# Regrouping the part-array matmuls of an attention round in a fused attention and expert kernel

## Chip, core and metric

The kernel runs on one core of a Trainium2 chip. The metric is the device time of one execution in microseconds (us); of several runs the median is given. The engines are TensorE (PE; its weight loads are listed as PEld), VectorE (DVE), ScalarE (ACT), GpSimd (POOL) and SyncE (SP, which only issues transfers).

## What is computed

Banded attention feeds a layer in which each token goes to one of eight experts. All data are float32.

```python
# q, k, v: (8 batches, 8 heads, 576 positions, 64); heads 0-3 plain window, heads 4-7 dilated
scores = q @ k.T / sqrt(64)
seen   = (0 <= i - j < 32)                                   # heads 0-3
seen   = (0 <= i - j < 128) and (i - j) % 4 == 0             # heads 4-7
x      = softmax(where(seen, scores, -1e9)) @ v              # -> (4608 tokens, 512)
logits = x @ w_gate                                          # (4608, 8)
e      = argmax(logits);  gate = softmax(logits)[e]
out    = gate * (relu(x @ w1[e]) @ w2[e])                    # w1[e]: 512x1024, w2[e]: 1024x512
```

## The kernel before

**Attention.** A unit is one pair of heads of one batch: 32 units, four to a batch, the first two of plain heads (`ty` 0), the last two of dilated ones (`ty` 1). A head's 576 queries are cut into nine blocks of 64, each with a band of 96 keys, so the matmuls are small and use only part of the 128x128 array of TensorE. A unit passes through these functions:

- `turn` (L293): transposes of q and of k into `turned`; a copy to qT on VectorE (L302), to kT on ScalarE (L304).[...]
- `front` (L340): 18 products of 64x64 weights with 96 columns (L360) into two banks `scores`. For the first four batches (`EARLY`), four matmuls put the mask into the banks ahead of them (L348), and VectorE takes the minimum from PSUM (L376); for later batches it adds the mask while it copies (L382, L389).
- `exponentials` (L393): nine or ten exponentials on ScalarE, with their sums.
- `norm` (L407): two small VectorE instructions, then a product on GpSimd (L412).
- `weights` (L416): nine transposes of the normed weights, three copies `eT` on VectorE (L424).[...]
- `summed` (L428), in two parts: 16 to 20 products with v, weights 96x64 (L437), into `xo`; ScalarE copies them to `xT` (L451, L458). An entry of the trace is half such a product[...], so a part shows 16 or 20 entries.
- `row_part` (L511): six transposes of `xT` into `xrow`[...], copied to `rows` by ScalarE and VectorE, then three products for the logits, weights 128x32 (L533).

`attention` (L463) is a software pipeline over rounds `i`. Round `i` holds, in this order: weights of unit i-2; norm of unit i-1; front of unit i; turns of unit i+1; rows and logits of unit i-3; exponentials of unit i; both parts of the sums of unit i-2. Matmuls of different kinds alternate through it. The next loads of q and k (`load_qk`) follow the turns and those of v (`load_v`) the sums, on SyncE's queue, which also issues the expert weights.

**Experts.** After the last unit of a batch, `route` (L541) finds each token's expert and writes its row to a bucket in memory; `tables` plans the slots of 128 rows that are then full. A slot (`moe`) is 32 products of 128x128 `ph` (L1183), each two entries in the trace, and eight of 128x512 `py` (L1215), likewise, with weights of 4 MB that SyncE fetches ahead. `xt` (L1108) is a turn of its rows.

**What sets the order.** `attention` and `moe` are generators. At each `yield cost, ended` of attention, the loop at the end hands out expert pieces by a clock of planned costs: `owed` grows with the cost times a rate, set from the slots that a routed batch makes ready, with due times from `ATT` = 32 and `BEHIND` = 12 (L1259). `ended` names a batch whose routing can begin. A round's costs sum to 6.6. Between two yields no expert piece is planned. A tile framework then orders the instructions of each engine by these priorities and by when it expects buffers and operands, so the built order departs here and there from the written one. All matmul results share seven PSUM banks.

## Time and profile before

| | |
|---|---|
| runs | 809.9, 810.85, 822.75 us; median 810.85 us |
| profiled execution | 815.9 us, its span 814.1 us |
| mean granted TensorE clock | 0.976 |
| PE, PEld busy | 766.0 us (94%), 559.6 us (69%) |
| DVE, ACT, POOL busy | 288.8 us (35%), 226.3 us (28%), 147.8 us (18%) |
| first, last sums (L437) | 31.1 us, 513.7 us |
| expert products ph, py busy | 274.3 us, 261.2 us |
| moved by transfers | 195.40 MB |

Busy is the time in which an engine executes. Matmuls overlap in the pipeline and their ends are modelled, so the time from the start of one group to the start of the next says more than a group's own duration. A timeline row gives start, duration, engine, line, tiles, weights and moving sizes, the count, and in brackets idle time ahead of it with what released it. The granted clock is the share of full speed that TensorE ran at.

### The profile page before, as it was taken

The page shows a single profiled execution, that of the slowest core. Times are in us where ns is not written, and L with a number is a line of the kernel's source. Part 1 is how long each engine was busy: PE and PEld are TensorE (multiplying, and loading weights), DVE is VectorE, ACT ScalarE, POOL GpSimd, SP SyncE. Part 2 cuts the span into 40 slices and gives each one's busy share as a digit, 9 for nine tenths or more (in the row PEclk, how much of TensorE's full clock was granted, in tenths as well). Part 3 has the DMA queues.
Part 4 walks back from the last instruction along what each step waited for, and adds up shares of the span by engine and source line. Part 5 has one row for each costly group of instructions (what it writes and reads, how often), then busy time and mean ns, then how long its engine had stood idle before and what let it go on. Part 6 is the DMA issues. An engine that isn't in the chain of part 4 may idle for free.

```text
span 814.1 us, 18002 instructions
## 1 busy us (share of the span) xinstructions
PE 766.0 (94%) x6838; PEld 559.6 (69%) x6838; DVE 288.8 (35%) x964; ACT 226.3 (28%) x853; POOL 147.8 (18%) x141
## 2 busy tenths in 40 slices
PE   4899978999999999999999999999999998999992
PEld 3777767777677777777777777776776472686770
DVE  2578857446333433336332452281010110111010
ACT  1687655343332333332322321100000000000100
POOL 0225423213111221113111130160000000000002
PEclk9699989999999999999999999999999999999997
DMA  9768799898998869968247477799980683883994
GB/s 209 168 139 214 182 304 305 189 305 278 307 268 316 292 217 308 297 205 269 71 147 248 143 210 263 253 362 350 323 283 27 217 273 130 311 279 135 316 330 159
DMA packets 165836, 195.40 MB, mean 240 GB/s; under 512 B 73520, under 2 KB 87600, under 8 KB 165746
## 3 DMA queue, kind: packets, MB, share of 16 engines
q1 hardware_dynamic: 153156, 169.00, 68.4%
q0 software_dynamic: 6992, 19.71, 6.7%
q10 hardware_dynamic: 5598, 5.48, 2.5%
q8 instruction: 57, 0.93, 0.5%
q14 instruction: 33, 0.27, 0.1%
HBM read 216.14 MB, written 22.59 MB: 293 GB/s over the span
## 4 chain that ended last, share of the span: by engine, by line
PE 44%; issue 36%; DMA 8%; DVE 5%; POOL 3%; ACT 3%; POOLq 0%; SPq 0%; ACTq 0%; DVEq 0%
PE ph L1183 13%; PE py L1215 12%; DMA x<-bucket 4%; PE xo L437 4%; PE weights L422 3%; PE scores L360 3%; POOL out_dram L1230 2%; ACT e L397 2%; PE xrow L523 2%; PE turned L319 2%; PE logits L533 1%; PE turned L311 1%; DMA k<-in_k_dram 1%; PE xt L1108 1%; DMA out_dram<-y,to 1%
## 5 line engine op out<-in xcount | busy, mean ns | idle before, releaser
L1183 PE MATMUL ph<-xt,w 128*128 128x128 f32 x2240 | 274.3, 277 | 0.0
L1183 PEld LDWEIGHTS ph<-xt,w 128*128 128x128 f32 x2240 | 261.6, 192 | 17.3 <-issue 14.4
L1215 PE MATMUL py<-w,h 128*128 128x512 f32 x560 | 261.2, 603 | 1.3 <-DVE h L1203 1.1
L1215 PEld LDWEIGHTS py<-w,h 128*128 128x128 f32 x560 | 99.3, 191 | 96.6 <-issue 89.4
L1230 POOL DMA_INDIRECT out_dram<-y,to x36 | 35.9, 998 | 376.7 <-ACT y L1226 356.1
L1226 ACT ACTIVATE y<-py,x 128x512 f32<-128x512 f32 x36 | 24.7, 685 | 228.4 <-PE py L1215 183.0
L412 POOL TENSOR_TENSOR e<-e,rec 128x864 f32<-128x864 f32 x32 | 52.2, 1631 | 170.0 <-DVE rec L411 103.7
L1110 DVE COPY xt<-xt 128x512 f32<-128x512 f32 x38 | 26.2, 690 | 151.1 <-PE xt L1108 151.0
L397 ACT ACTIVATE e<-e,lo 128x96 f32<-128x96 f32 x144 | 52.0, 363 | 73.9 <-DVE lo L389 73.6
L424 DVE COPY eT<-weights 96x384 f32<-96x384 f32 x96 | 48.7, 547 | 56.0 <-PE weights L422 55.2
L397 ACT ACTIVATE e<-scores,lo 128x96 f32<-128x96 f32 (+1 forms) x160 | 52.1, 344 | 28.1 <-DVE lo L376 21.2
L223 POOL DMA_INDIRECT bucket<-rows,idx x48 | 44.6, 930 | 54.5 <-DVE idx L622 32.6
L437 PEld LDWEIGHTS xo<-eT,v 96*64 96x64 f32 x1216 | 40.4, 140 | 18.9 <-issue 6.7
L437 PE MATMUL xo<-eT,v 96*64 96x64 f32 (+1 forms) x1216 | 46.8, 228 | 2.0 <-DVE qT L302 2.0
L1194 ACT ACTIVATE h<-ph 128x512 f32<-128x512 f32 x35 | 20.9, 597 | 89.5 <-PE ph L1183 83.3
L422 PE MATMUL weights<-ident,e 128*96 128x128 f32 x288 | 40.7, 291 | 3.4 <-POOL e L412 3.4
L422 PEld LDWEIGHTS weights<-ident,e 128*96 128x96 f32 x288 | 34.1, 135 | 9.3 <-issue 4.9
L1203 DVE TENSOR_SCALAR h<-ph 128x512 f32<-128x512 f32 x35 | 24.1, 690 | 40.9 <-PE ph L1183 40.8
L360 PEld LDWEIGHTS scores<-kT,qT 64*64 64x64 f32 x1152 | 33.8, 146 | 6.7 <-issue 3.8
L360 PE MATMUL scores<-kT,qT 64*64 64x96 f32 x1152 | 38.4, 265 | 0.0
L1227 DVE CAST to<-x 128x1 int32<-128x1 f32 x37 | 5.5, 149 | 92.7 <-DMA x<-bucket 78.0
L397 ACT ACTIVATION_READ_ACCUMULATOR e<-scores,lo 128x1 f32 (+1 forms) x160 | 33.3, 208 | 0.0
(210 smaller groups left out, 610.5 us busy)
## 6 DMA issues: line engine op xcount, KB each, us to landing
w<-in_moe_w_dram SPq DMA_DIRECT2D x164, 1024.0 KB
x<-bucket SPq DMA_DIRECT2D x26, 257.0 KB
v<-in_v_dram SPq DMA_DIRECT2D x32, 192.0 KB
q<-in_q_dram SPq DMA_DIRECT2D x32, 144.0 KB
q<-in_q_dram SPq DMA_DIRECT2D x8, 576.0 KB
v<-in_v_dram SPq DMA_DIRECT2D x48, 96.0 KB
k<-in_k_dram SPq DMA_DIRECT2D x28, 144.0 KB
k<-in_k_dram SPq DMA_DIRECT2D x7, 576.0 KB
```

Source lines behind the costliest of these rows:

```text
L223: nc.gpsimd.indirect_dma_start(out=bucket, out_offset=bass.IndirectOffsetOnAxis(ap=idx, axis=0), in_=rows, in_offset=None, bounds_check=NR ...
L360: nc.tensor.matmul(sc[r][64 * c : 64 * c + 64, 96 * (i % 5) : 96 * (i % 5) + 96], lhsT=qT[rows, 64 * j : 64 * j + 64], rhs=kT[rows, first_ ...
L397: nc.scalar.activation(out=e[p0:p1, i], in_=s[:, 96 * (i - i0) : 96 * (i - i0) + 96], func=AF.Exp, bias=lo[p0:p1, i : i + 1], scale=-1.0, ...
L412: nc.gpsimd.tensor_tensor(out=e, in0=e, in1=rec.unsqueeze(2).broadcast_to([128, 9, 96]), op=OP.mult)
L422: nc.tensor.transpose(tp[0:96, 128 * i : 128 * i + 128], e[:, a + i], ident)
L424: nc.vector.tensor_copy(eT, tp[0:96, 0:384])
L437: nc.tensor.matmul(xo[DH * h : DH * h + DH, at0 : at0 + nq], lhsT=vt[:, 2 * hl + r, j, :] if ty == 0 else vt[:, hl, j, DH * r : DH * r + D ...
L1110: nc.vector.tensor_copy(xt, ps)
L1183: nc.tensor.matmul(ph[:, fi], lhsT=w1[:, c, 128 * f : 128 * f + 128], rhs=xt[:, c], start=c == 0, stop=c == 3,)
L1215: nc.tensor.matmul(py, lhsT=h[:, f], rhs=w2[:, f], start=f == 0, stop=f == 7)
L1226: nc.scalar.activation(y, py, AF.Copy, scale=x[:, DM : DM + 1])
L1230: i = nc.gpsimd.indirect_dma_start(out=out, out_offset=bass.IndirectOffsetOnAxis(ap=to, axis=0), in_=y, in_offset=None, bounds_check=N - 1 ...
```

## The change

The order of a round in `attention` and the places of its yields. Now round `i` begins with norm of unit i-1, front of unit i, both parts of the sums of unit i-3 (a round later than before) and the logits of unit i-4, with no yield among them; then come weights of unit i-2, turns of unit i+1 and rows of unit i-3, and last the exponentials of unit i. `row_part` is split: its logits are a function of their own, `logit_part`, which runs a round after the rows. Routing of a batch begins behind its last logits. `load_v` goes with the sums. The planned costs become 3.0, 1.1, twice 0.5 and 0.65, together 5.75 a round; `ATT` and `BEHIND` stay. There are two rounds more, in which only the last units drain.

```diff
-        evs, dens, xT = {}, {}, None
-        for i in range(len(units) + LAG + 1):
-            if LAG <= i < len(units) + LAG:
-                eTs = weights(evs.pop(i - LAG))
-                yield 1.1, None
+        evs, dens, eTs, xTs = {}, {}, {}, {}
+        for i in range(len(units) + LAG + 3):
+            ended = None
             if 0 < i <= len(units):
                 norm(evs[i - 1], dens.pop(i - 1))
             if i < len(units):
                 evs[i], lo, places = front(qT["q"], qT["k"], units[i][1], units[i][0] < EARLY)
-            yield 1.1, None
+            u = i - LAG - 1
+            if 0 <= u < len(units):
+                b2, ty2, hl2 = units[u]
+                xTs[u] = pool.tile([128, S], F32, tag="xT", name="xT", bufs=3)
+                for part in range(2):
+                    summed(eTs[u], b2, xTs[u], ty2, hl2, part)
+                del eTs[u]
+                if hl2 == 1 and b2 + 1 < B:
+                    load_v(b2 + 1, ty2)
+            if 0 <= u - 1 < len(units):
+                b2, ty2, hl2 = units[u - 1]
+                logit_part(b2, 2 * ty2 + hl2, xTs.pop(u - 1))
+                ended = b2 if (ty2, hl2) == (1, 1) else None
+            yield 3.0, ended
+
+            if 0 <= i - LAG < len(units):
+                eTs[i - LAG] = weights(evs.pop(i - LAG))
+                yield 1.1, None
             if i + 1 < len(units):
...
                 for n in "qk":
                     qT[n] = turn(b2, ty2, hl2, n)
-                    yield 1.0, None
+                    yield 0.5, None
                 if hl2 == 1 and b2 + 1 < B:
                     load_qk(b2 + 1, ty2)
-            if i > LAG:
-                b2, ty2, hl2 = units[i - LAG - 1]
-                row_part(b2, 2 * ty2 + hl2, xT)
-                yield 0.9, b2 if (ty2, hl2) == (1, 1) else None
+            if 0 <= u < len(units):
+                b2, ty2, hl2 = units[u]
+                row_part(b2, 2 * ty2 + hl2, xTs[u])
+                yield 0.65, None
 
             if i < len(units):
                 dens[i] = exponentials(evs[i], lo, places)
-            if LAG <= i < len(units) + LAG:
-                b2, ty2, hl2 = units[i - LAG]
-                xT = pool.tile([128, S], F32, tag="xT", name="xT", bufs=3)
-                for part in range(2):
-                    summed(eTs, b2, xT, ty2, hl2, part)
-                    if part == 1 and hl2 == 1 and b2 + 1 < B:
-                        load_v(b2 + 1, ty2)
-                    yield 0.75, None
```

```diff
             )
+
+    def logit_part(b, c, xT):
         for j in range(3):
             nc.tensor.matmul(
                 logits[b][32 * j : 32 * j + 32],
```

## The prediction

> **What bounds the kernel now.** I read the page first, then the busy time by stretches, the waits, and the timeline of TensorE. On the page PE is busy 94% of the span, DVE 35%, ACT 28%, POOL 18%. The stretches say where that holds:

> ```profile
> 20.00:40.00 20.00, 16.60 (x190) 13.98 (x190) 10.95 (x30) 13.15 (x72) 4.90 (x3) 0.66 0.76 174
> 80.00:120.00 40.00, 34.22 (x530) 27.09 (x529) 30.07 (x101) 25.82 (x121) 14.63 (x13) 0.91 0.81 234
> 240.00:280.00 40.00, 40.00 (x352) 29.90 (x351) 13.57 (x41) 13.93 (x51) 5.23 (x4) 1.00 0.90 305
> 400.00:440.00 40.00, 40.00 (x365) 29.96 (x367) 13.49 (x30) 13.36 (x49) 5.25 (x4) 1.00 0.50 160
> ```

> The columns are the stretch, its length, busy us of PE, PEld, DVE, ACT and POOL, the granted clock, the DMA share and GB/s. Up to about 120 us attention runs alone, with DVE and ACT two thirds busy and PE with holes. From about 150 us on, expert slots stand between the attention pieces and PE never rests: what takes PE time off there shortens the span one for one, since ACT and DVE have two thirds of it free. Expert slots alone (from about 520 us) are full too.

> A busy PE is not PE at its best, so I take times from start to start. First the expert matmuls alone, then the same with attention among them:

> ```profile
> 561.84 3.74 PE L1183 MATMUL ph<-xt,w 128*128 128x128 f32 x32
> 565.42 7.03 PE L1215 MATMUL py<-w,h 128*128 128x512 f32 x16
> 572.29 2.95 PE L1183 MATMUL ph<-xt,w 128*128 128x128 f32 x25
> ```

> ```profile
> 299.83 0.80 PE L437 MATMUL xo<-eT,v 96*64 96x64 f32 x20
> 300.56 1.98 PE L1215 MATMUL py<-w,h 128*128 128x512 f32 x4
> 302.48 0.69 PE L437 MATMUL xo<-eT,v 96*64 96x64 f32 x16
> 303.09 2.84 PE L1215 MATMUL py<-w,h 128*128 128x512 f32 x6
> 305.77 1.15 PE L422 MATMUL weights<-ident,e 128*96 128x128 f32 x9
> ...
> 307.61 1.95 PE L1183 MATMUL ph<-xt,w 128*128 128x128 f32 x16
> 309.49 1.04 PE L360 MATMUL scores<-kT,qT 64*64 64x96 f32 x36
> 310.46 2.05 PE L1183 MATMUL ph<-xt,w 128*128 128x128 f32 x16
> 312.35 0.60 PE L1108 MATMUL xt<-ident,x 128*128 128x128 f32 x4
> ```

> Undisturbed, ph costs 3.58/32 = 0.112 us each and py 6.87/16 = 0.429. So the four py between two groups of sums should take 1.72 and take 1.92 (300.56 to 302.48): 0.20 more. The six with sums on one side alone take 2.68 against 2.57: 0.10 more. The sixteen ph ahead of the scores take 1.88 and those behind them 1.89, against 1.79: 0.09 and 0.10. A visit of TensorE to matmuls that use part of the array (scores 64x64, sums 96x64, logits 128x32), from full-array work and back, thus costs about 0.195 us over the groups themselves. Ahead of small transposes the way back is cheaper, about 0.045: turned, q and k after scores, 1.045 against 0.994.

> [...] ahead of xt the first load starts at 312.24, 0.11 us before its matmul, ahead of the scores both start at 309.49. [...] by stretches of 3.4 us the granted clock is 0.50 from 23.9 to 37.5 us, after an idle of 3.40 us, and at 105.8, 116.1 and 140.0, each after an idle of 2.0 to 2.4 us. [...] a one-row DVE instruction (L817) lasts 2.30 us at 100.46, over POOL's product at 101.08.

> **The change part by part.** No matmul, copy or transfer is added or removed. I counted groups in the built order of both programs.

> 1. Visits fall from 111 to 51. From round 17 on (expert slots between) from 71 to 32: 39 x 0.195 = 7.6 us, on the path, as PE is 100% busy. Before that, 40 to 19, at 0.093 + 0.045: 21 x 0.138 = 2.9 us.
> 2. Both halves of the sums together. Alone they take 0.73 and 0.61 (above); together x36 takes 1.20 where apart 0.705 + 0.615 = 1.32: 0.12 saved. Groups of sums fall from 50 to 36, 13 of these 14 after round 16: 1.6 us.
> 3. Logits no longer split around the row transposes. A split pair costs 0.443 where six in one group cost 0.456, so each split is almost a whole group more. Groups fall from 39 to 33, nearly all early: 6 x 0.445 = 2.7 us.
> 4. Inside the new visit the mode still changes (64x64, 96x64, 128x32). Logits to sums stands in the early rounds:

> ```profile
> 73.52 0.53 PE L533 MATMUL logits<-xT,wg 128*32 128x192 f32 x6
> 73.98 1.36 PE L437 MATMUL xo<-eT,v 96*64 96x64 f32 x40
> 75.33 1.19 PE L422 MATMUL weights<-ident,e 128*96 128x128 f32 x9
> ```

>    Logits take 0.456 ahead of sums as ahead of full work (0.456), and sums 1.29 to 1.35 behind them: no extra. Scores to sums isn't shown; its extra lies between 0 and a visit's 0.195 on 29 places (5.7 us). I take 0, by that neighbour.
> 5. Sums come a round later than their weights' transposes, logits a round after the sums. Their copies are then long done: the two waits of PE for an xT copy (2.4 and 0.5 us) can go. I count nothing. Routing follows a round later, and with it on POOL's queue a batch's six bucket writes (93.94 to 101.08), with one product held behind them, as before: nothing either.
> 6. Transposes behind the visit: the key copies on ACT, which the next scores need, now stand behind 6 to 8 exponentials of the same round and both xT copies; before, behind one or so. In the expert rounds (over 20 us each) that is covered. In the attention-only rounds: from the end of the scores, 0.85 until the first sums reach ACT, 8 x 0.315 + 2 x 0.35 = 3.2, key copies 0.7, scores 0.97 and a hand-over 0.1: 5.8 us a round. PE alone needs 1.0 turns + 1.0 weights + 0.66 rows + 0.46 + 1.29 + 1.17 = 5.6. The scores' starts show 6.2, 6.5, 6.1, 6.1, 6.5 before. ACT then takes back part of items 1 and 3, worth 5.6 early; I count 3 of it, bounds 0 and 5.6.
> 7. Start: PE idles 3.40 us (24.79, for POOL's product) and runs at half clock to 37.6. Scores now stand ahead of that wait and fill part of it; against that the first sums leave a stretch with holes and come when PE is full (1.2 us). Taken as 0, bounds a loss of 1.2 and a gain of 6.4 (the 12.8 us of half speed run at full).
> 8. SP's queue: x and the first eight weight loads (8.4 MB) move from ahead of batch 4's first q and k to behind them, still ahead of batch 3's second v. Before, PE loses about 12 us here (three idles of 2.4, 1.1, 2.0 and three windows at half clock). Now the sums of unit 14, in round 17, can wait for v: at the 300 GB/s seen around, 10 MB from about 107 us end near 140, and the sums are due near 133. About 7 us idle and two slow windows: again 10. Taken as 0, 6 either way.
> 9. The planner's costs are 5.75 a round against 6.6 with the same due times, so it gives less expert work to attention: at the last attention matmul 17 slots are done in the built order, 18 to 19 before. PE's sum is the same; the longer tail is as full (40.00 of 40 at 560 to 600, at 330 GB/s), and 24 slots are known before the last routing, so its later end stays covered.

> Sum: 7.6 + 1.6 + 3.0 = 12.2 us. The profiled execution took 815.9 us for a span of 814.1; I expect about 802 of that. The median of the runs is 810.85, so 798.6; I say 798.5.

> **Rivals.**
> - A. The start keeps its clock: as forecast, less 6.4: 792. For it: PE's idle before the first weights shrinks to about 2 us. Against: idles of 2.0 us elsewhere did halve the clock.
> - B. Mode changes inside the visit cost as much as outside: 5.7 us back, 804. Against it stands item 4.
> - C. Slower: ACT and DVE become the bound of the 14 attention-only rounds. If query or key copies get behind exponentials[...] and a round takes 7.5 instead of 6.25, that is 17.5 us lost against 9.2 kept: 819. It decides from 6.9 a round. For it: the ACT order of item 6 and two thirds busy DVE and ACT; against: 5.8 by my sum.
> - D. The v loads wait out the weights with PE empty, as in item 8 at its worst and with a colder clock: 10 lost, 808.

> **How the numbers follow.** Forecast 0.50, A 0.20, B 0.12, C 0.13, D 0.05. The forecast's own range is 792 to 805 (items 6 to 8). Low 785 takes A with good early rounds, high 815 the milder half of C. About 2% is what a measurement of this kernel can tell from no change: below 794.6 lie most of A and three tenths of the forecast, 0.32; above 827 a third of C, 0.04; the rest, 0.64.

> **What would show it.** In the profile after: about 51 visits; scores, sums, logits back to back and about 2.7 us together; ph and py between them at 0.112 and 0.429 with one pair of 0.1 a round; attention-only rounds at 5.7 to 5.9 (C: 7); the second expert stretch still full; half clock after 23.9 us or not (A); sums of unit 14 waiting for v or not (D). I am wrong if scores ahead of sums take more than 0.97, or if PE shows holes in the expert rounds.

## The result and the profile after

The changed kernel takes 819.53 us (median of four runs, 819.1 to 820.6), the kernel before beside it on the same chip 812.46: ratio 1.010, 95% interval 1.006 to 1.014. Instead of 12 us faster it is about 1% slower. Its profiled execution took 819.1 us with a span of 817.4 and a mean granted clock of 0.970; that is 3.3 us above the profiled span before, which lay some 3 us over its own median.

The lines of the changed program stand 12 lower where experts are concerned (py L1227, ph L1195, xt L1120, h L1215, the index cast `to` L1239). The busy time by stretches, columns as before (stretch, length, busy us of PE, PEld, DVE, ACT, POOL, granted clock, DMA share, GB/s):

```profile
20.00:40.00 20.00, 17.36 (x294) 14.43 (x288) 13.64 (x41) 17.75 (x94) 6.53 (x4) 0.91 0.68 167
80.00:120.00 40.00, 35.02 (x596) 29.59 (x596) 31.43 (x111) 30.00 (x145) 15.68 (x14) 0.96 0.80 212
180.00:200.00 20.00, 13.83 (x143) 11.30 (x142) 8.12 (x38) 5.77 (x23) 8.37 (x9) 0.80 1.03 342
240.00:280.00 40.00, 38.53 (x367) 29.20 (x366) 19.81 (x75) 13.35 (x51) 8.96 (x10) 1.00 1.04 343
400.00:440.00 40.00, 40.00 (x385) 31.33 (x384) 18.21 (x49) 13.72 (x50) 5.26 (x4) 1.00 0.52 160
520.00:560.00 40.00, 28.80 (x157) 20.38 (x157) 12.52 (x81) 1.98 (x4) 11.71 (x12) 0.83 0.74 261
```

From 400 to 440 us PE is as full as before. The holes are in two stretches that were full or nearly so in the kernel before:

```profile
180.00:200.00 20.00, 20.00 (x199) 15.74 (x198) 13.04 (x55) 6.27 (x26) 7.27 (x7) 1.00 0.85 275
...
520.00:560.00 40.00, 38.72 (x211) 26.74 (x210) 20.22 (x142) 3.50 (x6) 16.43 (x17) 1.00 0.96 339
```

From 520 to 560 us the expert slots stand alone; this is the later end that I had called covered.

Next PE's timeline, the visit of one round among expert work:

```profile
311.54 1.88 PE L1227 MATMUL py<-w,h 128*128 128x512 f32 x4
313.36 1.04 PE L360 MATMUL scores<-kT,qT 64*64 64x96 f32 x36
314.33 1.36 PE L437 MATMUL xo<-eT,v 96*64 96x64 f32 x40
315.62 0.53 PE L545 MATMUL logits<-xT,wg 128*32 128x192 f32 x6
316.07 1.98 PE L1227 MATMUL py<-w,h 128*128 128x512 f32 x4
317.89 3.73 PE L1195 MATMUL ph<-xt,w 128*128 128x128 f32 x32
```

This is as drawn: scores 0.97 ahead of sums, sums 1.29, logits 0.45, 2.71 together, and 0.10 over 1.72 for the four py on each side.

To see where time was won and lost I keep a ledger for every kernel: the time so far less the undisturbed price of every matmul that has started (ph 0.112, py 0.429, scores 0.024, sums 0.030, and so on; 741.2 us in all, the same in each kernel). What is left is the excess. Its growth by stretches, in us, one profiled execution a column, with the experiments told below:

| us | before | after | E5 | E6 | E7 | E9 | E10 | E12 |
|---|---|---|---|---|---|---|---|---|
| 0 to 40 | 27.2 | 24.3 | 24.8 | 23.7 | 24.3 | 23.3 | 24.3 | 24.3 |
| 40 to 180 | 35.1 | 35.0 | 33.8 | 35.2 | 35.2 | 37.1 | 42.3 | 37.4 |
| 180 to 210 | 4.6 | 10.0 | 11.6 | 6.8 | 2.7 | 9.9 | 2.9 | 1.3 |
| 210 to 520 | 22.0 | 11.8 | 15.9 | 13.1 | 20.5 | 10.8 | 18.8 | 11.9 |
| 520 to 560 | 1.9 | 14.4 | -0.3 | 0.1 | 0.1 | 11.9 | 0.0 | 0.0 |
| 560 to the end | -17.9 | -19.3 | -23.2 | -23.3 | -23.5 | -18.2 | -23.3 | -23.3 |
| span | 814.1 | 817.4 | 803.8 | 796.8 | 800.5 | 816.0 | 806.2 | 792.8 |

In the last stretch the slots that mix two experts are overpriced, so only differences count there. The change won 10.2 us between 210 and 520 us and 2.9 at the start, nothing from 40 to 180, and lost 5.4 us at 180 to 210 and 12.5 at 520 to 560. What PE waits for names both losses (releaser, us in total, times, longest):

```profile
PE py L1227 <- DVE h L1215: 11.2, 1, 11.2
PE xt L1120 <- DMA x<-bucket: 7.6, 2, 6.2
...
PE rank L615 <- DVE before L602: 5.0, 3, 2.0
...
PE lg L561 <- DVE lgs L558: 2.5, 3, 0.9
PE rank L608 <- DVE gate L622: 2.3, 2, 1.2
```

The first two of these before:

```profile
PE xt L1108 <- DMA x<-bucket: 2.3, 2, 1.4
...
PE py L1215 <- DVE h L1203: 1.1, 2, 0.6
```

One wait of 11.2 us in a stretch without attention is the largest change in the profile, so I followed it back. PE's py waits for VectorE's eviction of h, slot 19's second half:

```profile
541.54 6.37 PE L1227 MATMUL py<-w,h 128*128 128x512 f32 x8 [11.20 <-DVE h L1215]
```

VectorE's timeline there:

```profile
528.49 0.14 DVE L1000 TENSOR_TENSOR scratch<-exs,scratch 1x2 f32<-1x2 f32 x1
538.80 0.15 DVE L1239 CAST to<-x 128x1 int32<-128x1 f32 x1 [10.17 <-DMA out_dram<-y,to]
...
540.82 0.67 DVE L1215 TENSOR_SCALAR h<-ph 128x512 f32<-128x512 f32 x1
```

The eviction is not slow. It stands in VectorE's order behind a cast of one column, the output rows of slot 21, two slots ahead. (That the framework placed it so early because it expected the operand early is my reading; nothing here shows it.) The cast writes one of three index buffers, and that buffer is held until slot 18's rows have been scattered to the output. The scatter is on POOL's queue:

```profile
515.25 0.92 POOL L223 DMA_INDIRECT bucket<-rows,idx  x1 [8.99 <-DVE idx L634]
...
532.96 0.97 POOL L1242 DMA_INDIRECT out_dram<-y,to  x1 [0.31 <-issue]
```

Slot 18's result was ready at 520.1 (ScalarE's y at 519.41, 0.69 long). But the last routing had begun its burst of fourteen bucket writes at 515.25, some 1.27 us apart, and the scatter goes out behind them, 12.9 us late; its data land by 538.8, the cast runs, then the eviction, then PE. The same view of the kernel before:

```profile
527.48 0.98 POOL L1230 DMA_INDIRECT out_dram<-y,to  x1 [16.73 <-ACT y L1226]
528.77 0.92 POOL L223 DMA_INDIRECT bucket<-rows,idx  x1 [0.31 <-issue]
```

There a scatter slips out 1.3 us ahead of the burst, and the next goes out behind the burst at 546.55, 3.1 us after its slot's result is ready. The burst is as long (17.78 us against 17.71 in the changed kernel); only its place in the 14.45 us of a slot has changed. On this the chain from queue to queue is shown; that the buffer and the cast are its links was tested next. VectorE's timeline shows the hold: PE's second ph group of slot 19 had ended at 526.90 (523.16, 3.74 long), yet between 528.63 and 538.80 VectorE ran nothing, and both the 128x512 eviction and the small instructions of the tables came behind the 128x1 cast. In this idle of 11.2 us PE's granted clock went to 0.50, from 533.3 to 547.0 us, so that the eight py entries that begin at 541.54 take 6.21 us until the next group where their price is 3.43. 11.2 + 2.8 is nearly all of the 14.4 us that the tail's excess grows by.

### The profile page after: what moved, and what is told of

It reads as the page before. It is cut to its first block, busy times and chain, and to the rows that moved or that the text cites. A ratio compares the mean times of both kernels' runs of the same rounds, so it can differ in the third digit from the quotient of the medians.

```text
span 817.4 us, 18022 instructions
## 1 busy us (share of the span) xinstructions
PE 751.2 (92%) x6838; PEld 559.4 (68%) x6838; DVE 288.3 (35%) x964; ACT 225.2 (28%) x853; POOL 147.2 (18%) x141
## 4 chain that ended last, share of the span: by engine, by line
PE 43%; issue 32%; DMA 9%; ACT 6%; DVE 5%; POOL 2%; POOLq 0%; SPq 0%; ACTq 0%; DVEq 0%
PE py L1227 14%; PE ph L1195 14%; DMA x<-bucket 5%; ACT e L397 4%; PE xo L437 3%; PE scores L360 2%; PE weights L422 2%; POOL out_dram L1242 2%; DMA v<-in_v_dram 2%; PE xrow L531 2%; DMA k<-in_k_dram 2%; PE turned L319 1%; PE xt L1120 1%; PE turned L311 1%; PE logits L545 1%
## 5 line engine op out<-in xcount | busy, mean ns | idle before, releaser
L1195 PEld LDWEIGHTS ph<-xt,w 128*128 128x128 f32 x2240 | 263.5, 193 | 19.1 <-issue 18.1
L1195 PE MATMUL ph<-xt,w 128*128 128x128 f32 x2240 | 272.6, 277 | 0.0
L1227 PE MATMUL py<-w,h 128*128 128x512 f32 x560 | 257.3, 602 | 11.2 <-DVE h L1215 11.2
L1227 PEld LDWEIGHTS py<-w,h 128*128 128x128 f32 x560 | 101.5, 192 | 114.7 <-issue 99.5
L1238 ACT ACTIVATE y<-py,x 128x512 f32<-128x512 f32 x36 | 24.7, 686 | 269.3 <-PE py L1227 224.1
L397 ACT ACTIVATE e<-e,lo 128x96 f32<-128x96 f32 x144 | 51.8, 362 | 16.0 <-DVE lo L389 12.8
L437 PE MATMUL xo<-eT,v 96*64 96x64 f32 (+1 forms) x1216 | 43.2, 224 | 1.5 <-DMA v<-in_v_dram 1.5
L1239 DVE CAST to<-x 128x1 int32<-128x1 f32 x37 | 5.5, 148 | 110.4 <-DMA x<-bucket 82.6
L437 PEld LDWEIGHTS xo<-eT,v 96*64 96x64 f32 x1216 | 38.7, 138 | 7.4 <-issue 1.9
L304 ACT COPY kT<-turned 128x288 f32<-128x288 f32 x64 | 23.1, 414 | 72.6 <-PE turned L311 55.0
L422 PE MATMUL weights<-ident,e 128*96 128x128 f32 x288 | 39.3, 284 | 1.0 <-POOL e L412 1.0
L360 PE MATMUL scores<-kT,qT 64*64 64x96 f32 x1152 | 37.6, 262 | 0.6 <-ACT kT L304 0.5
L302 DVE TENSOR_SCALAR qT<-turned 128x288 f32<-128x288 f32 x64 | 26.5, 448 | 32.2 <-PE turned L311 17.5
L422 PEld LDWEIGHTS weights<-ident,e 128*96 128x96 f32 x288 | 32.7, 131 | 7.0 <-issue 4.8
L360 PEld LDWEIGHTS scores<-kT,qT 64*64 64x64 f32 x1152 | 32.4, 143 | 7.4 <-issue 5.0
```

What stands on the lines that cost most here:

```text
L302: nc.vector.tensor_scalar(out, in_, -SCALE, None, op0=OP.mult)
L360: nc.tensor.matmul(sc[r][64 * c : 64 * c + 64, 96 * (i % 5) : 96 * (i % 5) + 96], lhsT=qT[rows, 64 * j : 64 * j + 64], rhs=kT[rows, first_ ...
L397: nc.scalar.activation(out=e[p0:p1, i], in_=s[:, 96 * (i - i0) : 96 * (i - i0) + 96], func=AF.Exp, bias=lo[p0:p1, i : i + 1], scale=-1.0, ...
L422: nc.tensor.transpose(tp[0:96, 128 * i : 128 * i + 128], e[:, a + i], ident)
L437: nc.tensor.matmul(xo[DH * h : DH * h + DH, at0 : at0 + nq], lhsT=vt[:, 2 * hl + r, j, :] if ty == 0 else vt[:, hl, j, DH * r : DH * r + D ...
L1195: nc.tensor.matmul(ph[:, fi], lhsT=w1[:, c, 128 * f : 128 * f + 128], rhs=xt[:, c], start=c == 0, stop=c == 3,)
```

## The experiments

All ratios are against the kernel before on the same chip. E1 to E4 ran on one chip (before 816.38 us), E5 to E8 on a second (812.11), E9 to E12 later on that second chip (812.32).

**E1 and E2: six index buffers, in the changed kernel and in the one before.**

```diff
-                to = mpool.tile([128, 1], I32, tag="to", name="to", bufs=3)
+                to = mpool.tile([128, 1], I32, tag="to", name="to", bufs=6)
```

> The changed kernel with six buffers in place of three for the 128x1 index tile; nothing else. Theory (late index): near the end of attention TensorE stands 11.2 us because the cast that fills the index of a later slot waits for an index buffer, whose scatter stands on GpSimd's queue behind 14 bucket writes, and the eviction of the slot's second half stands behind that cast on VectorE. Then the idle time and the window at half clock behind it go: 12 to 16 us off, about 805 us, 1% below the kernel before. Rival (the stretch lacks weights or the tables of the last batch): the idle time stays, the time stays at 818 to 821 us.

> The kernel before with six buffers for the index tile. Theory: there the bucket writes fall right behind a scatter, TensorE waits less than 1.5 us in this stretch, so the time stays within 2 us of the kernel before. Rival (the index tile holds up both kernels alike): it gains as much as the changed kernel does, 10 us or more, and then the regrouping itself would be worth nothing.

E1: 815.4 us, ratio 0.998 (0.995 to 1.000), short of the 805 expected. E2: 817.38 us, 0.999 (0.996 to 1.002), no gain, as expected. So the buffer is a link: the growth from 520 to 560 falls from 14.4 to 6.7 us in E1. But only half went. In E1's trace the cast, at 535.72, waits 2.38 us for its slot's rows (`x`) instead, still ahead of the eviction, which starts at 538.17, and PE loses 3.76 us. The buffer was the longest of two strings; what ties either to PE is the cast's place in the queue. E2's trace, of an execution 5 us over its median, shows that second string in the old order too: a cast waits 7.78 us for rows, and PE idles 3.99 us at 557.41, where the kernel before lost 1.1 us around here.

**E3: E1 with rows asked for earlier.**

```diff
-        x = xs[j] = mpool.tile([128, ROW], F32, tag="x", name=f"x_{j}", bufs=3)
+        x = xs[j] = mpool.tile([128, ROW], F32, tag="x", name=f"x_{j}", bufs=4)
...
-        x = (j, "x", 0, 2 * j - 2)
+        x = (j, "x", 0, 2 * j - 4)
```

> As e1, and the rows of a slot are asked for half a slot's products earlier, with four row buffers in place of three. Theory (the rows stand behind 4 MB of other loads at 181 us): the wait of 6.2 us for rows at about 190 us shrinks to under 2 us and with it the half clock up to 202 us: 6 to 10 us below e1, about 797 us. Rival (that stretch is bound by bytes moved, so what is not waited for here is waited for at the next load): within 2 us of e1.

813.53 us, 0.994 (0.990 to 0.998), only 1.9 us below E1: by its time the rival. The wait for rows near 190 us falls to 2.35 us (E1: 8.58), but others of 1.23 and 3.91 come at 216 and 281, and the tail still loses 4.85 us at 535 behind the cast. Earlier rows help at 196 us, and don't cure the tail.

**E4: E1 with the visit taken apart.** Yields of 0.9, 0.75, 0.75 and 0.6 between scores, halves of the sums and logits, in place of 3.0 behind all: 94 visits and 51 groups of sums, against 51 and 36.

```diff
                 xTs[u] = pool.tile([128, S], F32, tag="xT", name="xT", bufs=3)
+                yield 0.9, None
                 for part in range(2):
                     summed(eTs[u], b2, xTs[u], ty2, hl2, part)
+                    yield 0.75, None
...
+            else:
+                yield 2.4, None
...
-            yield 3.0, ended
+            yield 0.6, ended
```

> As e1, with yields between scores, the two parts of the sums and the logits, their planned costs still 3.0 together, so that expert pieces stand between them again: 94 visits to part-array work in place of 51, and 51 groups of sums in place of 36. Theory (a visit costs 0.195 us, a group of sums 0.12): 43 x 0.195 + 15 x 0.12 = 10 us above e1. Rival (the gain between 210 and 520 us comes from the order of buffers and queues, not from visits): within 3 us of e1.

825.07 us, 1.010 (1.008 to 1.013), 9.7 us above E1; the excess grows by 20.0 us from 210 to 520, nearly the 22.0 of before. It also waits 12.93 us for a q near 138, so that its time agrees with the 10 us forecast is partly chance; E10 repeats it.

**E5: the cast behind the second eviction of its own slot,** with three buffers as in the changed kernel.

```diff
-                    nc.vector.tensor_scalar(h[:, 4:8], ph, 0.0, None, op0=OP.max)
+                    second = nc.vector.tensor_scalar(h[:, 4:8], ph, 0.0, None, op0=OP.max)
...
-            nc.vector.tensor_copy(to, x[:, DM + 1 : ROW])
+            with tc.issue_after(second.ins):
+                nc.vector.tensor_copy(to, x[:, DM + 1 : ROW])
```

(and the same for the eviction of a mixed slot)

> The changed kernel with one edge more: the cast of a slot's index column is ordered behind the second eviction of h of its own slot, so that it can no longer stand in front of the eviction of an earlier slot. TensorE's order is unchanged. My theory (the last burst of bucket writes delays a scatter, the cast of a slot two ahead waits for that scatter's buffer in VectorE's queue, and the eviction that TensorE needs stands behind the cast): the wait of 11.2 us at 541 us and its 13.7 us of half clock are gone, the excess between 520 and 560 us falls from 14.5 to 2 to 4 us, the time to 10 to 13 us below the changed kernel, 806 to 810 us. Rival (the eviction was late because the slot's rows or weights come late anyway, the cast only hides it): the wait stays, as one for x or w, at 5 us or more, and the time stays above 813 us.

802.31 us, 0.987 (0.982 to 0.993): lower than I expected. The tail's loss is gone. VectorE's timeline:

```profile
533.29 0.67 DVE L1215 TENSOR_SCALAR h<-ph 128x512 f32<-128x512 f32 x1
533.88 0.13 DVE L1240 CAST to<-x 128x1 int32<-128x1 f32 x1
```

POOL's burst is where it was (516.36 to 534.08) and a scatter still waits for its end, but now nobody on PE's path waits for that scatter; PE is busy 40.00 of 40 us from 520 to 560. What surprised me lies past 560 us: 3.9 us less there as well.

**E6 and E7: cast and early rows together, in the changed kernel and in the one before.** The edits of E5 and of E3's rows, three index buffers.

> The same, and each slot's rows are asked for two halves of a slot earlier, with a fourth buffer for them. By my theory both new waits of the changed kernel (6.2 us at 196 us for rows, 11.2 us at 541 us) are cured, and what is left is the gain of the regrouped rounds: 16 to 20 us below the changed kernel, 800 to 804 us, 0.98 to 0.985 of the kernel before, faster than both. Rival (earlier rows only move the wait to the queue they are issued on, or to another slot): 806 us or more.

> The kernel before with the same two repairs. My theory: it loses 1.4 us for rows and about 1.1 us on these waits, so it gains at most 4 us: 0.995 to 1.0 of the kernel before. Rival (the repairs are worth as much without the regrouping, and the regrouping brought nothing): 0.98 to 0.985, as fast as the changed kernel with both.

E6: 797.42 us, 0.982 (0.976 to 0.988). E7: 801.14 us, 0.986 (0.981 to 0.992). E6's ratio is in the range expected, its time 2.6 us below it; E7 is a miss, 11 us gained where I gave it 4, and its ratio is close to the rival's 0.98 to 0.985. The kernel before had the same fault in a place that I had not counted, ahead of the mixed slots; its VectorE timeline:

```profile
687.49 0.15 DVE L1227 CAST to<-x 128x1 int32<-128x1 f32 x1 [16.90 <-DMA x<-bucket]
687.60 0.69 DVE L1175 TENSOR_SCALAR hrow<-ph 128x512 f32<-128x512 f32 x1
```

PE waits 2.2 us for this eviction at 688 and 1.2 at 641, and the clock is 0.50 from 689.5 to 692.9 us; the row from 560 us on shows 5.6 us less in E7. So most of E6's gain belongs to the repairs and not to the regrouping. The difference of E7 and E6 is 3.7 us by the medians, with overlapping intervals: these two alone don't exclude that the regrouping brings nothing. In E6 PE still waits 6.1 us for rows, in E7 for none.

**E8: the order of before at the change's pace.** Only the costs are scaled, from 6.6 to 5.75 a round.

```diff
-                yield 1.1, None
+                yield 0.96, None
...
-                    yield 1.0, None
+                    yield 0.87, None
...
-                yield 0.9, b2 if (ty2, hl2) == (1, 1) else None
+                yield 0.79, b2 if (ty2, hl2) == (1, 1) else None
...
-                    yield 0.75, None
+                    yield 0.65, None
```

> The kernel before with its order of sub-steps as it was and only their costs scaled from 6.6 to 5.75 us a round, as the change has them: 17 instead of 18 slots stand ahead of the last attention matmul, at 109 visits. If the pace alone (fewer slots done, the last routing meeting another slot) makes the new wait in the expert rounds near 540 us: a hole of 5 us or more there, and 1.01 to 1.02 of the kernel before. If it takes the later sums, logits and routing too: no such hole, 0.995 to 1.005.

816.16 us, 1.004 (1.002 to 1.006), in the range of the second alternative. The burst starts at 520.11, just behind a scatter at 518.77, as in the kernel before. There is a smaller hole of 2.03 us at 545.8, where a cast waits 5.31 us for rows. Fewer slots done ahead of the end do not by themselves move the burst.

**E9: the order of the change at the pace of before.**

```diff
-            yield 3.0, ended
+            yield 3.4, ended
...
-                yield 1.1, None
+                yield 1.25, None
...
-                    yield 0.5, None
+                    yield 0.6, None
...
-                yield 0.65, None
+                yield 0.75, None
```

> The changed kernel with its groups of sub-steps as they are, and their costs scaled back from 5.75 to 6.6 us a round (47 visits, 18 instead of 17 slots done ahead of the last attention matmul, as in the kernel before). In TensorE's order the ranks of the last routing then stand 12 ph matmuls and the 8 py matmuls of a slot ahead of that slot's end, some 4.8 us, nearly as in the changed kernel (8 ph and 8 py, 4.3 us); in the kernel before they stand just behind a slot's py matmuls. Theory A (the place of the last routing in its slot makes the tail's wait, and the later groups put it there, whatever the pace): a hole of 8 us or more in the expert rounds between 530 and 565 us, and 812 to 820 us. Theory B (the pace makes it): no hole over 2.5 us there, and 800 to 806 us.

819.8 us, 1.009 (1.006 to 1.011): theory A, by time and by place. VectorE's timeline:

```profile
551.60 0.15 DVE L1239 CAST to<-x 128x1 int32<-128x1 f32 x1 [10.78 <-DMA out_dram<-y,to]
...
553.81 0.67 DVE L1215 TENSOR_SCALAR h<-ph 128x512 f32<-128x512 f32 x1
```

PE idles 9.55 us at 554.53. The burst starts at 527.33, the slot's result is ready at 534.7 and its scatter goes out at 544.92. With 18 slots done as in the kernel before, the wait is there again: it goes with the order and not with the pace. (By the traces the last ranks start 10.1 us ahead of their slot's end here and 9.3 in the changed kernel; the 4.8 and 4.3 of my expectation are too short by half.)

**E10: both repairs, the visit taken apart** (E4's yields in E6; 92 visits and 51 groups of sums against 57 and 36).

> The changed kernel with both repairs (the cast behind its own slot's eviction, rows earlier), and with the round's groups taken apart again: a yield between scores, the halves of the sums, and the logits, 92 visits and 51 groups of sums in place of 57 and 36. My price of a visit, 0.195 us late and 0.138 early, and 0.12 us for a group of sums, give 6 to 9 us more than the same kernel with the groups together (797.4 us): 803 to 807 us, and 6 to 9 us more growth of the excess between 210 and 520 us, 19 to 22 instead of 13.1. Rival (the visits cost little once the waits are cured): under 801 us, under 16 us of growth.

809.38 us, 0.996 (0.994 to 0.998), 12 us above E6 and above the 803 to 807 expected. Part of that is not the visits: it waits 12.0 us for a q at 136 us (40 to 180: 42.3 against 35.2). From 210 to 520 us no idle of PE is over 0.4 us, and the excess grows by 18.8 us. In E6 it grows by 13.1, of which 2.8 is a wait for rows, in E12 by 11.9, of which 1.3: 10.3 and 10.6 without. So taking the groups apart costs 8.2 to 8.5 us there, inside the 6 to 9 of my prices, although 18.8 itself lies just under the 19 I gave.

**E11: the kernel before with the cast repaired, nothing else.**

> The kernel before with the cast behind its own slot's second eviction, and nothing else. With the rows earlier as well it had lost 11 us, where I had expected 4 at most: I had counted the two waits near 540 and 554 us (1.1 us), and not the two ahead of the mixed slots (1.2 us at 641, 2.2 us at 688, with 1.7 us of half clock), where the same cast stands ahead of an eviction. By this count the cast is worth 5 to 6 us, the rows 2.3, and the start's clock, which differs between executions, the rest: 804 to 808 us. Rival (the rows are worth most of it): 809 us or more.

806.11 us, 0.993 (0.990 to 0.995), as counted: 6.2 us below before. Rows still cost it 3.23 us at 207.

**E12: both repairs and the pace of before** (E9's costs in E6; 46 visits).

> The changed kernel with both repairs and the costs scaled back to 6.6 us a round: 46 visits, one slot more done ahead of the last attention matmul. If the pace's only harm lay in the two waits, nothing is left of it: 796 to 800 us, as at 5.75 (797.4). If the faster pace leaves the early stage short of cover, or slots ask for rows too early at the slower one: 792 to 795, or over 802 us.

793.66 us, 0.975 (0.968 to 0.982), the fastest of all and in the lower range of the second alternative. Its busy time by stretches:

```profile
180.00:200.00 20.00, 20.00 (x195) 15.67 (x195) 13.75 (x57) 6.48 (x25) 8.20 (x8) 1.00 0.93 312
520.00:560.00 40.00, 40.00 (x224) 28.52 (x223) 17.77 (x125) 3.26 (x5) 15.52 (x16) 1.00 1.03 362
```

PE waits 2.2 us for rows in all, against 6.1 in E6. The intervals of E6 and E12 overlap, so that the slower pace is better once repaired is likely, and not settled. Against E7, which has the same planned pace, it is 7.7 us shorter by the spans and 7.5 by the medians: what the regrouping brings when neither long new wait is there. All four runs of E12 (790.0 to 796.6) lie below all four of E7 (799.4 to 802.3), though the intervals of their ratios just touch.

## Why the prediction was wrong

**Items 1 and 2, fewer visits and joined sums late: right.** 7.6 + 1.6 = 9.2 us were forecast. From 210 to 520 us the traces show 55 visits and 29 groups of sums before, 16 and 13 after, which is 39 x 0.195 + 16 x 0.12 = 9.5 us at the same prices; the change won 10.2 there, with repairs in both kernels 20.5 - 11.9 = 8.6 (E7, E12), and taking it apart again cost 8.2 to 8.5 (E10).

**Item 3 and the early part of item 1: counted 3.0, found 0.1** (40 to 180 us). The plain attention-only rounds take 5.1 to 6.4 us by the scores' starts, 6.0 on average against 5.8 in item 6 and 6.2 before; rival C's 7 did not come. But the rounds that route a batch take 10.3 and 12.0 us where they took 9.0 and 9.4. Logits, routing's transposes and ranks now stand close together on PE, with VectorE's short steps between them: PE's waits for these (the lines for rank and lg above) are 5.0 + 2.5 + 2.3 = 9.8 us against 2.8 + 1.1 = 3.9 before. Those 5.9 us and a new wait of 1.5 us for v eat what the visits gave and the three waits of 2.4, 2.0 and 2.0 us (for an xT copy, for qT, for L817 on VectorE) that stand here before and are gone after. That this is where the gain went is read from the waits; no run moved it.

**Item 4, no extra where the shapes change inside the visit: right,** 0.97 for the scores, 1.29 for the sums, 0.45 for the logits; rival B falls.

**Item 5, "and with it on POOL's queue a batch's six bucket writes ...: nothing either": the step that failed, with item 9.** It counted the writes and not when they start, and for the last batch not the eight writes of blanks behind them. Fourteen writes hold POOL's queue for 17.7 us, more than a slot's 14.45, and a scatter was caught in each of the four traces compared here; whether it is caught by 3.1 us (before) and 3.9 (E8) or by 12.9 (after) and 10.2 (E9) went in these traces with how far the ranks of the last routing stand from a slot's end. In the built order they come just behind a slot's py before, and 8 ph and 8 py ahead of a slot's end after (12 and 8 in E9).

**Item 9, "the longer tail is as full ..., so its later end stays covered": wrong,** 12.5 us. I took the tail's fullness from a stretch behind the burst (561 us on), and covered meant slots known, not buffers free. The pace, which the item was about, does little (E8, E9).

**Item 7, the start: within its bounds,** 2.9 us won, half clock for 3.4 us after 24.7 instead of 13.7 from 23.9. Rival A thus came in part, but E7 and E11, with the old order and the same idle of 3.2 to 3.5 us for POOL's product, also show 3.4 us. It differs between executions, so these traces don't show that the change did it.

**Item 8, SP's queue: within ±6, by another transfer.** (The "about 12 us" that it gives the kernel before sum to 10.6: 5.5 of idle and half of 3 x 3.4.) Sums waited 1.5 us for v, not 7 (rival D falls). The late one was a slot's rows, PE's timeline and then SP's:

```profile
196.20 1.08 PE L1120 MATMUL xt<-ident,x 128*128 128x128 f32 x4 [6.17 <-DMA x<-bucket]
```

```profile
166.84 10.43 SPq L282 DMA_DIRECT2D v<-in_v_dram  x13
...
181.30 0.38 SPq L1058 DMA_DIRECT2D x<-bucket  x1
```

They are issued behind thirteen loads of v that keep SP for 10.4 us, and land about 15 us later in a stretch with the DMA engines full (share 1.03). That the loads of v are what delays them is read from the order of the queue; no run moved those loads. A half-clock time of 10.2 us goes with it. E3, E6 and E12 shrink the loss with earlier rows; the pace of before alone (E9) does not. It was 5.4 us, and the one term of item 8 that I had not named.

In sum, by the profiled spans: -2.9 at the start, -0.1 early, +5.4 at 180 to 210, -10.2 in the middle, +12.5 in the tail, -1.4 behind it: +3.3 us, where -12.2 was forecast. By the medians the change costs 7.1; the other 3.8 us are that the profiled execution before lay 3.4 above its median and the one after 0.4 below, and no stretch can be given for them. No rival held the case: the one that ended slower (C) named the wrong engines and the wrong end of the kernel, and that its 819 is the measured time is chance.

## What to carry to other kernels

Before a change shifts the order on one engine, look at what stands at the head of the other engines' queues: here a cast of 0.15 us, whose buffer came late, held all that stood behind it on VectorE for 10.17 us, and PE lost 11.2. Such a wait can be long while PE feels little of it (16.90 us for rows at one place before the change, of which PE lost 2.2) until the phase shifts. Where a burst on a queue is longer than the period of the work that it delays, read from the built order at which phase it starts; "covered" has to be said of buffers as well as of work. And when a change wins what it should on its path and the time doesn't follow, repair the new wait in both kernels before judging the change: here that gave 0.986 without it, 0.982 with it, 0.975 with it at the pace of before, and 1.010 for the change alone.
